# Attention and two MoE layers on one core: a longer transfer latency in the ordering model, own slots for the last old sums, and new early priorities

## The chip, the cores and the metric

The kernel runs on one core of one Trainium2 chip. The metric is the device time of one execution in microseconds. Three runs of the kernel before gave 543.34, 543.43 and 543.93 us; the median is 543.43 us.

## What is computed

Causal attention over 2 batches, 12 heads, 448 positions and head size 64, then two feed-forward blocks on the 896 tokens. Weights arrive in 64-bit floats for the matrices, and the work is done in pairs of fp32r parts (a high and a low part, three matmuls for one product).

```python
def reference(**kwargs):
    ...
    attn_out = _attn_ref(**attn_kwargs)              # softmax(q k^T / 8, causal) v
    x = np.ascontiguousarray(attn_out.transpose(0, 2, 1, 3)).reshape(B * S, H * D)   # 896 x 768
    x = _moe_ref(x=x, **moe_kwargs)                  # ((x w1) * (x w2)) w3 w_out
    return _moe2_ref(x=x, **moe2_kwargs)             # h = x w_in;  (h * clip(h + 3, 0, 6) / 6) w_out
```

Sizes: w1 and w2 are 768 x 1024, w3 is 1024 x 1024, the first w_out 1024 x 768, w_in 768 x 2048, the second w_out 2048 x 768.

## The kernel before

**Stages.** (1) Attention in 12 units (batch, pair of heads): scores (`s`, L539), the running minimum (`max`, DVE L551), exponent (`exp`, ACT L555), scaling (POOL L574), transposes (`ptp`, L597) with their copy out (ACT L602), product with v (`o`, L614). Beside it the product w3 w_out (`pw`, L683, 16 banks of 24 matmuls of 384 columns), which goes to DRAM (`product_of`). (2) `pa` (L831): x w1 and x w2 by Strassen's seven products. (3) `px` (L947): (a * b) times the product of stage 1. (4) eight `pg` groups (L831; x2 w_in, hard swish, 63 matmuls each) with `po` groups between them (`collected`, L1083, 48 matmuls each), whose partial sums go to DRAM and come back (`sums_of`: stored at L798, loaded at L1078). (5) `joined`: the last three `po` groups, 42 matmuls each by Strassen's products, which load the old sums once more (L1042), add (L1046) and store the output (L1050).

**Weights.** A unit of 64-bit weights is fetched by SP (`fetch`, L331, into `raw`, `raw2` or a slot beside), and turned into fp32r parts by `convert`: `bits` (ACT L361, ACT L364 or DVE L368, DVE L371), in Strassen groups `combine` (DVE L439), and `split` (ACT L341 or POOL L337, DVE L343).

**The order.** Every operation is an entry of `Plan` with an engine, a cost, what it reads and writes, and a rank. `Plan.issue` plays the entries through a small model of the engines: an operation is ready when what it needs has ended, plus a latency (0.2 us behind PE, 2.4 us behind a transfer on SP), and each engine takes the ready operation of lowest rank. The order so found is the order in each engine's instruction stream; on the chip each engine executes its stream in that order and waits at whatever is not there yet. PE also prefers to stay with the kind of its last operation for `RUN[kind]` operations. In attention the rank is the unit's number plus an offset of `RANK`; the fetch of weight unit n has rank `PACE * n`, its conversion `PACE * n + 1` up to the last unit of w3 (n = 15; units 0, 5, 6 are w3, 1 to 4 and 7 to 10 w_out, 11 to 15 w3). The `pw` products have rank 50 and up; late stages have `DENSE + n`, with `AHEAD` = 2.39 on top for a conversion. The evictions of `pw` have rank `EVICT`, the sums that `pa` needs (`difference`, `moving`) rank `FORM`. `FILL` = 60 transposes of nothing (L640) have rank 1000 and go where the model sees PE with nothing else.

**Slots of the last part.** `joined(i)` loads four tiles of old sums, o[m, b]. In groups i = 0 and 2 they take slots of the tags `c22` (b = 0) and `a2` (b = 1), two slots each; in group 1 of `a1` and `r`. `collected` takes `c22` and `a2` for its own sums. A slot is free when the tile that held it has been stored. The tiles `T1_0` to `T2_2` of `tp` hold the moving operands of `pg` and are last read by the eighth `pg` group.

Of the kernel before, what the change touches and what calls it, by code (L numbers as in the profile page):

```python
# [16 lines left out]

RANK = {'load': -0.56, 'max': -1.83, 'exp': -9.0, 'pt': 0.3, 'pv': 1.3}  # L20

BANKS = {'s': 3, 'pt': 2, 'o': 1}
DENSE_BANKS = 2
# [3 lines left out]
AHEAD = 2.39  # L27

BESIDE = 50.0
PACE = 0.74  # L30

EVICT = -8.56

POOLED = ("wr", "w3")
DENSE = 100.0
# [12 lines left out]

ASIDE = 48

THIRD = 0.969 * 2.0 ** -29, -0.26

FORM = -7.3

WARM = 13

LATER = 2.97

UP = 1

# [1 line left out]

FILL, IDLE = 60, 1000.0

RUN = {'r': 4, 'f': 7, 'q': 11}
TURN = {("q", "f"): 0.17, ("q", "r"): 0.15, ("q", "c"): 0.1, ("f", "q"): 0.09, ("r", "q"): 0.09, ("c", "q"): 0.1, ("f", "r"): 0.1, ("f", "c"): 0.09, ("r", "c"): 0.09, ("c", "f"): 0.17, ("c", "r"): 0.15}
SHAPE = (2, 12, 448, 64)
DFF, DFF2 = 1024, 2048
# [20 lines left out]
class Plan:  # L89
# [8 lines left out]
    def __init__(self):  # L98
        self.ops = []
        self.tags = {}  # L100
        self.ports = set()
        self.kinds = {}

    def tile(self, make, tag, bufs, after=()):
        return Handle(self, make, tag, bufs, after)
# [24 lines left out]
    def issue(self):  # L130
        n = len(self.ops)
        deps = [set(o[3]) for o in self.ops]
        order = set()
        for bufs, hs in self.tags.values():
            for x, h in enumerate(hs):
                first = h.uses[0][0]
                if x >= 1:
                    before = hs[x - 1].uses[0][0]
                    if before not in deps[first]:
                        order.add((before, first))  # L140
                    deps[first].add(before)
                if x >= bufs:
                    deps[first].update(u[0] for u in hs[x - bufs].uses)
                deps[first].update(h.after)
                deps[first].discard(first)
                for u in h.uses:
                    if u[0] != first:
                        if first not in deps[u[0]]:
                            order.add((first, u[0]))
                        deps[u[0]].add(first)  # L150
        after = [[] for _ in range(n)]
        for i in range(n):
            for j in deps[i]:
                after[j].append(i)
        left = [len(d) for d in deps]
        ready = [0.0] * n
        engines = {o[0] for o in self.ops}
        coming = {e: [] for e in engines}
        here = {e: [] for e in engines}
        free = {e: self.START.get(e, 0.0) for e in engines}  # L160
        for i in range(n):
            if not left[i]:
                heapq.heappush(coming[self.ops[i][0]], (0.0, i))
        busy, locked = None, 0.0

        def settle(i, end):
            e = self.ops[i][0]
            for j in after[i]:
                near = self.ops[j][0] == e and (e != "sp" or (i, j) in order)
                ready[j] = max(ready[j], end + (self.CHAIN.get(e, 0.0) if near else self.LATENCY.get(e, 0.15)))  # L170
                left[j] -= 1
                if not left[j]:
                    heapq.heappush(coming[self.ops[j][0]], (ready[j], j))

        kind, run = "f", 0
        todo = n
        while todo or busy:
            t, e = min((
                (free[e] if here[e] else max(free[e], coming[e][0][0]), e)
                for e in engines if here[e] or coming[e]  # L180
            ), default=(float("inf"), None))
            if busy and busy[1] <= t:
                settle(*busy)
                busy = None
                continue
            while coming[e] and coming[e][0][0] <= t:
                i = heapq.heappop(coming[e])[1]
                heapq.heappush(here[e], (self.ops[i][4], i))
            same = [x for x in here[e] if self.kinds[x[1]] == kind] if e == "pe" and run < RUN.get(kind, 0) else None
            if same:  # L190
                i = min(same)[1]
                here[e].remove(min(same))
                heapq.heapify(here[e])
            else:
                i = heapq.heappop(here[e])[1]
            self.ops[i][2]()
            todo -= 1
            cost = self.ops[i][1]
            if e == "pe":
                cost += TURN.get((kind, self.kinds[i]), 0.0)  # L200
                run = run + 1 if kind == self.kinds[i] else 1
                kind = self.kinds[i]
            if e == "pool":
                free[e] = max(t, locked) + cost
                busy = i, free[e]
                continue
            free[e] = t + cost
            if i in self.ports:
                locked = free[e]
                if busy:  # L210
                    free["pool"] = busy[1] + cost
                    busy = busy[0], free["pool"]
            settle(i, free[e])
        return max(free.values())


@with_exitstack
def attention_moe_moe2(ctx: ExitStack, tc, q, k, v, w1, w2, w3, w_out, v_in, v_out, out):
# [683 lines left out]
    second(KF - 1)  # L902

    x2 = {}

    def differences(p, ps, rank):

# [123 lines left out]
    def joined(i):  # L1031
# [1 line left out]
        n = first_of["po", c, i]  # L1033
        rank = DENSE + n
        X, Y, Z = (dense_bank(f"po{a}{i}") for a in "XYZ")
        o = {}
        for m in (0, 1):
            for b in range(B):
                name = f"o{c}_{m}_{b}_{i}"
                o[m, b] = scratch(("a2", "r")[i % 2], name) if b else scratch("a1", name) if i % 2 else spare(name)  # L1040
                t, at_ = o[m, b], (i + HK * m, b)
                plan.op("sp", 0.6, lambda t=t, at_=at_: nc.sync.dma_start(t[:, :], sums_of[at_]),  # L1042
                        reads=[summed.at(at_)], writes=[t], rank=rank - 2)

        def add(x, bank, stored=None):
            plan.op("dve", dve(S), lambda: nc.vector.tensor_tensor(x[:, :], bank[:, :S], x[:, :], ALU.add),  # L1046
                    reads=[bank], writes=[x], rank=rank)
            if stored:
                m, b = stored
                plan.op("sp", 0.6, lambda: nc.sync.dma_start(  # L1050
                    out[(i + HK * m) * P:(i + HK * m + 1) * P, cols(b)], x[:, :]), reads=[x], rank=rank)

        multiply(i, "P1", X, True, rank, "vo")
        add(o[0, 0], X)
        multiply(i, "P2", Y, True, rank, "vo")
        add(o[0, 0], Y, (0, 0))
        multiply(i, "P6", X, False, rank, "vo")
        add(o[0, 1], X)
        multiply(i, "P5", Z, True, rank, "vo")
        add(o[1, 1], Z)  # L1060
        multiply(i, "P7", X, False, rank, "vo")
        add(o[1, 1], X, (1, 1))
        multiply(i, "P3", Z, False, rank, "vo")
        add(o[0, 1], Z, (0, 1))
        multiply(i, "P4", X, False, rank, "vo")
        add(o[1, 0], X, (1, 0))

    def collected(c, i):
        n = first_of["po", c, i]
# [90 lines left out]
```

## Time and profile before

| | |
|---|---|
| median of three runs | 543.43 us |
| the profiled execution | 544.48 us, its span 542.6 us |
| PE busy | 530.2 us (98%) |
| DVE, ACT, POOL busy | 409.3, 306.0, 114.6 us |
| DMA | 87.18 MB, 161 GB/s over the span |

The span is the time from the first to the last instruction of the program in one profiled execution; some 1.9 us lie around it. PE is TensorE, PEld its weight loads, DVE VectorE, ACT ScalarE, POOL GpSimd, SPq the queue of SyncE, which here issues every transfer. PE counts as busy from the start to the modelled end of a matmul, and matmuls overlap, so a busy share near 100% can hide a slow rate: the starts of successive matmuls tell the rate. In a row of the timeline the bracket tells how long the engine had been idle before the instruction, and what ended that.

### The profile page before, as it was taken

Reading aid. Unit: us, or ns where it says so; the run is one execution under the profiler, and the core shown is the slowest. Engines: PE = TensorE matmul, PEld = TensorE weight load, DVE = VectorE, ACT = ScalarE, POOL = GpSimd, SP = SyncE. Lnnn points to the kernel's source line nnn. Section 1 sums busy time; section 2 is a strip of 40 time slices with the busy share of each in tenths; the row PEclk is TensorE's granted clock in tenths of the full one; section 3 lists DMA queues with packets and bytes.
Section 4 is the critical chain, followed back from the end, with each engine's and each line's share of the span. In section 5 each row is a group of like instructions: output and inputs, shape, how many; then the busy total and the mean of one; then the engine's idle time right before and its main releaser. Section 6 shows DMA issues by size and latency. Waiting matters only on the chain.

```text
span 542.6 us, 8387 instructions
## 1 busy us (share of the span) xinstructions
PE 530.2 (98%) x3031; PEld 468.4 (86%) x3031; DVE 409.3 (75%) x780; ACT 306.0 (56%) x597; POOL 114.6 (21%) x156
## 2 busy tenths in 40 slices
PE   9999999999999999999999999998999999999997
PEld 6657777778999999999999999997999889999886
DVE  4998989464686888987555678997757795899564
ACT  4787878776634555645434257986646542576000
POOL 3767874443021111110000120101020000000000
PEclk9999999999999999999999999998999999999999
DMA  7877775431422333333412105545563747462763
GB/s 253 307 231 231 303 240 205 156 98 30 151 62 110 116 117 126 144 125 132 175 37 80 56 4 185 220 158 165 185 210 127 267 165 233 171 209 88 229 198 131
DMA packets 33513, 87.18 MB, mean 161 GB/s; under 512 B 3264, under 2 KB 23488, under 8 KB 30912
## 3 DMA queue, kind: packets, MB, share of 16 engines
q1 hardware_dynamic: 33472, 86.65, 46.9%
q8 instruction: 23, 0.38, 0.3%
q14 instruction: 18, 0.15, 0.1%
HBM read 72.48 MB, written 14.16 MB: 160 GB/s over the span
## 4 chain that ended last, share of the span: by engine, by line
PE 71%; DVE 13%; ACT 7%; DMA 6%; issue 2%; POOL 1%; SPq 0%; DVEq 0%; POOLq 0%; ACTq 0%
PE pw L683 11%; PE px L947 11%; PE paX L831 11%; PE po L1083 10%; PE pgX L831 5%; PE paZ L831 5%; PE o L614 3%; PE paY L831 3%; PE s L539 3%; PE ptp L597 2%; PE pgZ L831 2%; DVE prb L551 2%; PE poX L831 2%; DMA vor<-in_moe_w_out 2%; DMA sums_of<-o 1%
## 5 line engine op out<-in xcount | busy, mean ns | idle before, releaser
L1083 PE MATMUL po<-g,vo 128*128 128x448 f32 x432 | 87.4, 362 | 0.0
L1083 PEld LDWEIGHTS po<-g,vo 128*128 128x128 f32 x432 | 81.0, 187 | 5.4
L683 PE MATMUL pw<-wr,w 128*128 128x384 f32 x384 | 73.3, 343 | 0.1
L683 PEld LDWEIGHTS pw<-wr,w 128*128 128x128 f32 x384 | 65.5, 188 | 7.2 <-issue 6.1
L574 POOL TENSOR_SCALAR prb<-prb,sums 128x64 f32<-128x64 f32 (+6 forms) x84 | 56.7, 692 | 44.4 <-DVE sums L568 24.6
L947 PE MATMUL px<-ab,wp 128*128 128x448 f32 x288 | 57.8, 362 | 0.0
L947 PEld LDWEIGHTS px<-ab,wp 128*128 128x128 f32 x288 | 54.0, 187 | 3.6
L555 ACT ACTIVATE prb<-prb,sums 128x64 f32<-128x64 f32 (+6 forms) x84 | 42.1, 502 | 21.1 <-DVE sums L551 20.6
L337 POOL TENSOR_SCALAR vja<-vir 128x768 fp32r<-128x768 f32 x8 | 9.1, 1134 | 166.5 <-DVE x2t L770 53.0
L551 DVE CUSTOM_DVE_ANT_0 prb<-s,maskb 128x64 f32<-128x64 f32 (+6 forms) x84 | 32.0, 415 | 12.7 <-PE s L539 11.2
L602 ACT COPY pt<-ptp 128x512 f32<-128x512 f32 x48 | 26.2, 585 | 8.9 <-PE ptp L597 8.8
L539 PE MATMUL s<-ks,qs 64*64 64x192 f32 (+6 forms) x336 | 30.3, 406 | 0.4 <-DVE sums L551 0.4
L597 PE MATMUL ptp<-ident,prb 128*128 128x128 f32 x120 | 24.7, 278 | 1.2 <-ACT pt L602 0.6
L775 ACT ACTIVATE rab<-q,consts 128x448 f32<-128x448 f32 x24 | 16.2, 674 | 16.1 <-DVE q L975 16.0
L614 PE MATMUL o<-pt,vr 128*64 128x448 f32 (+3 forms) x192 | 23.4, 386 | 0.0
L794 DVE TENSOR_TENSOR o<-po,o 128x448 f32<-128x448 f32 x24 | 14.9, 622 | 9.6 <-PE po L1083 4.7
L614 PEld LDWEIGHTS o<-pt,vr 128*64 128x64 f32 x192 | 12.7, 136 | 10.7 <-issue 5.5
L361 ACT ACTIVATE vor<-vor 128x1024 f32<-128x1024 f32 x12 | 14.0, 1164 | 13.3 <-DMA vor<-in_moe_w_out 13.3
L337 POOL TENSOR_SCALAR w2b<-w2r 128x768 fp32r<-128x768 f32 x8 | 9.3, 1165 | 54.4 <-DVE w2r L439 22.5
L597 PEld LDWEIGHTS ptp<-ident,prb 128*128 128x128 f32 x120 | 15.7, 140 | 4.4 <-ACT pt L602 1.4
L831 PE MATMUL pgX<-T3g,vjb 128*128 128x448 f32 x72 | 17.0, 384 | 2.5 <-ACT q L972 2.5
L597 PE MATMUL ptp<-swap,prb 128*128 128x128 f32 x72 | 18.0, 277 | 0.9 <-ACT pt L602 0.8
(184 smaller groups left out, 1181.5 us busy)
## 6 DMA issues: line engine op xcount, KB each, us to landing
vor<-in_moe_w_out SPq DMA_DIRECT2D x12, 1024.0 KB, 5.5
w3r<-in_moe_w SPq DMA_DIRECT2D x8, 1024.0 KB, 5.3
sums_of<-o SPq DMA_DIRECT2D x36, 224.0 KB, 3.0
o<-sums_of SPq DMA_DIRECT2D x36, 224.0 KB, 3.0
wrr<-in_moe_w_out SPq DMA_DIRECT2D x8, 768.0 KB, 6.4
w1r<-in_moe_w SPq DMA_DIRECT2D x8, 768.0 KB, 5.9
w2r<-in_moe_w SPq DMA_DIRECT2D x8, 768.0 KB, 4.4
vjr<-in_moe_w_in SPq DMA_DIRECT2D x8, 768.0 KB, 4.4
```

Source lines behind the costliest of these rows:

```text
L337: plan.op("pool", single(size), lambda: nc.gpsimd.tensor_scalar(hl[:, HI, at_:at_ + size], x(), 1.0, 1.0, ALU.mult, ALU.mult), reads=reads ...
L539: nc.tensor.matmul(ps[at_:at_ + T, :n], qs[u][T * j:T * j + T, t * T:(t + 1) * T], ks[u][T * j:T * j + T, :n], start=True, stop=True)
L551: plan.op("dve", dve(n), lambda: nc.vector.tensor_tensor_reduce(out=z(), in0=ps[:, :n], in1=maskb[:, S - n:], scale=-SCALE, scalar=3.0e38, ...
L555: plan.op("act", 0.29 + n * 0.00083, lambda: nc.scalar.activation(z(), z(), AF.Exp, bias=sm[:, 0, t:t + 1], scale=-1.0, accum_out=sm[:, 1, ...
L574: nc.gpsimd.tensor_scalar(s, s, sm[:, 1, t:t + 1], 1.0, ALU.mult, ALU.mult)
L597: nc.tensor.transpose(ps[:, i * P:(i + 1) * P], pb[:, OFF[t] + kb * P:OFF[t] + (kb + 1) * P], swap if t % 2 else ident)
L602: plan.op("act", act(4 * P), lambda: nc.scalar.copy(d[:, 4 * g:4 * g + 4].rearrange("p n h i -> p (n h i)"), ps[:, :]), reads=[ps], writes ...
L614: nc.tensor.matmul(ps[T * j:T * j + T, kb * P:S], vr[u][:, kb, j, :], d[:, base[kb]:base[kb] + TQ - 2 * kb, j, :], start=kb == 0, stop=kb ...
L683: nc.tensor.matmul(ps[:, :W], weight(n, a, kk), hls[m][:, c, at_:at_ + W], start=kk == 0 and a == c, stop=kk == KF - 1 and a == LO)
L831: nc.tensor.matmul(ps[:, :S], hl[:, a, off + kk * P:off + (kk + 1) * P], t[:, c, at_], start=first and kk == 0 and a == c, stop=kk == n - ...
L947: nc.tensor.matmul(ps[m, b][:, :S], weight(n, a, kk), ab[kk][:, c, cols(b)], start=kk == 0 and a == c, stop=kk == KF - 1 and a == LO)
L1083: nc.tensor.matmul(ps[:, :S], hls[n][:, a, at_:at_ + P], gt[k][:, d, cols(b)], start=kk == 0 and a == d, stop=kk == KC - 1 and a == LO)
```

## The change

Three things. In `Plan.issue`, a transfer on SP among the operations made after `plan.dense` (set behind the last `pa` group, so from `px` on) makes its dependents ready 4.0 us (`SLOW`) after its end in the model, where the latency was 2.4 us; what only follows in the SP queue's order keeps its rule. `joined` takes for its old sums the slots `T2_i` (m = 0) and `T1_i` (m = 1), each [P, 2, S] with the two batches side by side. And eight constants of the early part have new values: ranks in attention, `PACE`, `EVICT`, `FORM`, `LATER` (the rank of the loads of v), and `RUN`. The arithmetic, and the number of matmuls, are the same.

```diff
-RANK = {'load': -0.56, 'max': -1.83, 'exp': -9.0, 'pt': 0.3, 'pv': 1.3}
+RANK = {'load': -0.54, 'max': -3.0, 'exp': -7.72, 'pt': 0.75, 'pv': 1.25}
-PACE = 0.74
-EVICT = -8.56
+PACE = 1.21
+EVICT = -9.28
+SLOW = 4.0
-FORM = -7.3
+FORM = -14.03
-LATER = 2.97
+LATER = 3.56
-RUN = {'r': 4, 'f': 7, 'q': 11}
+RUN = {'r': 5, 'f': 6, 'q': 19}
...
+        self.dense = 1 << 30
...
                 near = self.ops[j][0] == e and (e != "sp" or (i, j) in order)
+                if e == "sp" and i >= self.dense and not near:
+                    ready[j] = max(ready[j], end + SLOW)
...
     x2 = {}
+    plan.dense = len(plan.ops)
...
-        o = {}
+        o = [plan.tile(lambda a=a: later["t"].tile([P, 2, S], F32, tag=f"{a}_{i}", name=f"o{c}_{a}_{i}"), f"{a}_{i}", 1, (done,))
+             for a in ("T2", "T1")]
         for m in (0, 1):
             for b in range(B):
-                name = f"o{c}_{m}_{b}_{i}"
-                o[m, b] = scratch(("a2", "r")[i % 2], name) if b else scratch("a1", name) if i % 2 else spare(name)
-                t, at_ = o[m, b], (i + HK * m, b)
-                plan.op("sp", 0.6, lambda t=t, at_=at_: nc.sync.dma_start(t[:, :], sums_of[at_]),
-                        reads=[summed.at(at_)], writes=[t], rank=rank - 2)
-
-        def add(x, bank, stored=None):
-            plan.op("dve", dve(S), lambda: nc.vector.tensor_tensor(x[:, :], bank[:, :S], x[:, :], ALU.add),
-                    reads=[bank], writes=[x], rank=rank)
+                plan.op("sp", 0.6, lambda t=o[m], b=b, at_=(i + HK * m, b): nc.sync.dma_start(t[:, b, :], sums_of[at_]),
+                        reads=[summed.at((i + HK * m, b))], writes=[o[m].at(b)], rank=rank - 2)
+
+        def add(m, b, bank, stored=False):
+            t = o[m]
+            plan.op("dve", dve(S), lambda: nc.vector.tensor_tensor(t[:, b, :], bank[:, :S], t[:, b, :], ALU.add),
+                    reads=[bank], writes=[t.at(b)], rank=rank)
...
         multiply(i, "P1", X, True, rank, "vo")
-        add(o[0, 0], X)
+        add(0, 0, X)
...
```

The other calls of `add` change in the same way.

## Rows read from the trace of the kernel before

**Rows 1.** Stretch: length, busy us (count) of PE, PEld, DVE, ACT, POOL; PEclk, DMA, GB/s.
```profile
0.00:57.00 57.00, 53.13 (x420) 36.20 (x421) 45.81 (x127) 41.82 (x110) 37.63 (x62) 1.00 0.76 261
...
370.00:380.00 10.00, 7.77 (x32) 6.75 (x31) 7.55 (x11) 5.96 (x9) 1.93 (x2) 0.83 0.34 112
```
**Rows 2.** Chain that ended last, stretches of one kind: start us, us, what.
```profile
116.48 1.88 PE o L614 x16
...
119.26 2.29 PE pw L683 x12
...
126.86 1.88 PE o L614 x16
...
138.82 21.00 PE pw L683 x120
...
260.61 57.60 PE px L947 x288
```
**Rows 3.** Timeline of the tail: start us, us, engine, line, tiles, [idle before].
```profile
510.96 1.36 PE L831 MATMUL poX<-g,voa 128*128 128x448 f32 x6
...
521.11 1.48 PE L831 MATMUL poZ<-g,voc 128*128 128x448 f32 x6 [1.10 <-DVE o L1046]
```
**Rows 4.** The chain in the tail.
```profile
514.05 2.84 DMA sums_of<-o
516.91 3.40 DMA o<-sums_of
...
537.65 1.22 PE poX L831 x6
```
**Rows 5.** Timeline around 375 us, PE and ACT.
```profile
371.08 1.97 PE L831 MATMUL pgZ<-T1g,vjb 128*128 128x448 f32 x9
...
373.63 1.18 ACT L361 ACTIVATE vor<-vor 128x1024 f32<-128x1024 f32 x1 [2.75 <-DMA vor<-in_moe_w_out]
...
375.29 3.17 PE L831 MATMUL pgX<-T3g,vjb 128*128 128x448 f32 x9 [2.23 <-ACT q L972]
...
382.38 1.96 PE L1083 MATMUL po<-g,vo 128*128 128x448 f32 x9
```
**Rows 6.** Timeline around 433 us, PE and ACT.
```profile
429.19 1.97 PE L831 MATMUL pgZ<-T1g,vjb 128*128 128x448 f32 x9
...
430.06 0.90 ACT L361 ACTIVATE vjr<-vjr 128x768 f32<-128x768 f32 x1 [1.08 <-DMA vjr<-in_moe_w_in]
...
437.74 3.56 PE L1083 MATMUL po<-g,vo 128*128 128x448 f32 x17
```
**Rows 7.** The chain at these two places: start us, us, what.
```profile
365.33 8.22 DMA vor<-in_moe_w_out
...
422.65 7.33 DMA vjr<-in_moe_w_in
```
**Rows 8.** Time to landing of the twelve vor transfers, 256 to 543 us.
```profile
DMA to landing us min/median/max: 4.7/5.5/8.2
```
**Rows 9.** PE's groups from 4.3 to 57 us: shapes, count, busy us, mean ns.
```profile
L539 PE MATMUL s<-ks,qs 64*64 64x128 f32 (+6 forms) x156 | 15.4, 423 | 0.4 <-DVE sums L551 0.4
...
L683 PE MATMUL pw<-wr,w 128*128 128x384 f32 x48 | 10.0, 350 | 0.1
...
L614 PE MATMUL o<-pt,vr 128*64 128x448 f32 (+3 forms) x64 | 7.8, 386 | 0.0
```
**Rows 10.** ACT's main groups in the first 60 us, columns as in rows 9.
```profile
L555 ACT ACTIVATE prb<-prb,sums 128x256 f32<-128x256 f32 (+6 forms) x39 | 19.9, 511 | 12.4 <-DVE sums L551 12.2
...
L602 ACT COPY pt<-ptp 128x512 f32<-128x512 f32 x20 | 10.9, 586 | 2.5 <-PE ptp L597 2.5
...
L361 ACT ACTIVATE wrr<-wrr 128x768 f32<-128x768 f32 x8 | 7.4, 930 | 0.0
...
L555 ACT ACTIVATION_READ_ACCUMULATOR prb<-prb,sums 128x1 f32 x39 | 7.3, 188 | 0.0
```

More of the change, by code (lines that the diff above doesn't have):

```diff
@@ L1048, in add @@
             if stored:
-                m, b = stored
                 plan.op("sp", 0.6, lambda: nc.sync.dma_start(
-                    out[(i + HK * m) * P:(i + HK * m + 1) * P, cols(b)], x[:, :]), reads=[x], rank=rank)
+                    out[(i + HK * m) * P:(i + HK * m + 1) * P, cols(b)], t[:, b, :]), reads=[t.at(b)], rank=rank)
         multiply(i, "P1", X, True, rank, "vo")
-        add(o[0, 0], X)
+        add(0, 0, X)
         multiply(i, "P2", Y, True, rank, "vo")
-        add(o[0, 0], Y, (0, 0))
+        add(0, 0, Y, True)
@@ L1057, in joined @@
         multiply(i, "P6", X, False, rank, "vo")
-        add(o[0, 1], X)
+        add(0, 1, X)
         multiply(i, "P5", Z, True, rank, "vo")
-        add(o[1, 1], Z)
+        add(1, 1, Z)
         multiply(i, "P7", X, False, rank, "vo")
-        add(o[1, 1], X, (1, 1))
+        add(1, 1, X, True)
         multiply(i, "P3", Z, False, rank, "vo")
-        add(o[0, 1], Z, (0, 1))
+        add(0, 1, Z, True)
         multiply(i, "P4", X, False, rank, "vo")
-        add(o[1, 0], X, (1, 0))
+        add(1, 0, X, True)
```

## The prediction

> **What bounds the kernel now.** I read the page first (engines, the 40 slices), then the chain that ended last, then busy time by stretch, then the timeline where PE had waited. PE is busy for 98% of the span, and the chain runs through PE for nearly all of the time from 57 to 330 us. So the question at each place is not who is busy but whether PE is fed at full rate, and the starts of matmuls tell that: 288 `px` matmuls of 448 columns take 57.60 us, 0.20 us each, and 120 `pw` matmuls take 21.00 us, 0.175 us each [rows 2]. The work of PE is the same before and after, so the change can only give back time in which PE ran below these rates. I find four such places.
>
> The tail: the three `joined` groups begin at 510.96 and the last matmul ends at 537.65 + 1.22 = 538.87 [rows 3, 4]. That is 27.9 us for 126 matmuls; at 0.20 us they need 25.2. Lost: 2.7 us. The chain shows why: a store of old sums takes 2.84 us, a load of old sums follows it for 3.40 us, DVE adds, and PE waits for the bank [rows 3, 4].
>
> Around 375 us: PE should have begun its next product 1.80 us after 371.08 and, three products of 1.80 us later, the `po` group at 378.3; it began at 382.38 [rows 5]. Lost: 4.1 us. ACT stood 2.75 us at the conversion of `vor`, and the copy that frees PE's bank was queued behind it. PE waited 2.23 us; then its clock, 0.83 over this window [rows 1], made the next nine matmuls take 3.17 us where 1.97 us is the row of an undisturbed nine [rows 5].
>
> Around 433 us, the same with a shorter wait: 429.19 + 4 x 1.80 = 436.39, begun at 437.74 [rows 6]. Lost: 1.35 us, at full clock. ACT stood 1.08 us at `vjr` with the copy behind it.
>
> The first 57 us: PE did some 5 units of attention (64 `o` matmuls are 4 units, 156 `s` matmuls 5.6) and 48 `pw` matmuls [rows 9]. At full rate one unit with two runs of 12 `pw` takes 126.86 - 116.48 = 10.38 us [rows 2], less 24 x 0.175 = 4.2: 6.2 us for the unit. So 5 x 6.2 + 8.4 = 39.4 us of the 52.7 us from 4.3 us on were useful, 13.3 us were lost (19 if I count 4 units, 10 if 5.6). The 60 filling transposes lie in there. From 57 us until `pw` ends PE has no such gap.
>
> **The change part by part.**
>
> *Own slots.* Before, group 0 of `joined` loads into `c22` and `a2`, behind the stores of the last `collected` group, which has the same slots. The last of these stores lands at 514.05 + 2.84 = 516.89, and the load starts at 516.91 [rows 4]. Now the slots are those of the moving operands of the eighth `pg` group, which are last read some 25 us before `joined` begins. The data of group 0 was stored some 20 us before. So the loads of groups 0 and 1 can land early. Group 2 really needs the last stores: 516.9 plus 3.4 us is 520.3, and its turn on PE comes at 511 + 2 x 8.4 = 527.8, so 7 us of cover remain. The loads now stand earlier in SP's queue, among the fetches and the stores of sums; a load that waits there for a store (up to about 3 us) holds what is queued behind, but by then the last weights are already issued, and the output stores behind it have no reader. What is late next is PE's own order, with one bank copied out during the next product of 1.2 us. Value: -2.7 us, with bounds -2.7 and 0.
>
> *A latency of 4.0 us.* The model gives a transfer its cost on SP (0.0035 us per column, 3.58 us for `vor`, 2.69 us for `vjr`) plus the latency. The old model expected `vor` 5.98 us after its start; it took 8.22 us [rows 7]. Put on the chip's clock, in the old model it lands at 371.3. The copy is ready when the product that ran up to the next one's start at 371.08 [rows 5] has drained and the model's 0.2 us are over, at about 371.5. So ACT took the conversion first. In the new model it lands 7.58 us after, at 372.9, 1.4 us behind the copy: ACT does the copy first, and PE goes on. That is -4.1 us, with bounds -4.1 and 0 (the model's clock need not run with the chip's). For `vjr` the new model says 6.69 us against 7.33 us [rows 7], that is 429.3; the copy for which PE waited is ready at about 429.4. This is a tie; I take half, -0.7 us, with bounds -1.35 and 0. A conversion that comes later in the order costs nothing as long as ACT or DVE has other work and the unit is needed only one group later (8 to 12 us of PE); if that cover goes, PE waits for weights, and the dearest row for such a wait is the 4.1 us. The whole late order is drawn anew by this, so I put in one new wait of the kind at 433 us, +1.4 us. Bounds for new waits: 0 and two of the kind at 375 us, +8.2.
>
> A rule speaks against the 4.0. The Trainium skill ("DMA: Bandwidth & Descriptors", Anatomy of one DMA) gives a transfer a constant part of about 2.0 us. By that rule 2.4 was already enough, the new figure only delays conversions in the order, and the value of this part would be 0. The trace agrees for the usual transfer: the median `vor` landed after 5.5 us [rows 8], 1.9 us over its cost. It differs for the two that hurt: 8.22 - 3.58 = 4.6 us and 7.33 - 2.69 = 4.6 us.
>
> *Early priorities.* `PACE` from 0.74 to 1.21 is the large one. Conversion n had rank 0.74 n + 1 beside units 0 to 11, and now has 1.21 n + 1: the fifth conversion, with which the first `pw` can run, goes from rank 4.0 to 5.8, the eleventh from 8.4 to 13.1, behind all of attention. `max` at -3.0 pushes DVE the same way. So attention goes ahead and `pw` starts later; fetches move with their conversions on SP, behind the loads of q, k and v. What attention alone gives PE is limited by ACT: per unit seven exponents with their reads, (19.9 + 7.3) / 39 x 7 = 4.9 us, and four copies, 2.2 us [rows 10], with one conversion of 0.93 us [rows 10] some 8.0 us, in which PE has 6.2 us of attention. The loss is 1.8 us per unit until `pw` fills it: for some 6 units 11 us, and some 3 us of start. That is 14 us against the 13.3 us before: 0, with bounds -4 (a loss of 9 us, near the smaller count above) and +13 (attention starves PE through all 12 units, 22 us, and 4 us of start). DVE's 45.8 busy us of 57 [rows 1] say the same: DVE has little left for more.
>
> *`RUN` r from 4 to 5.* A run of 12 `pw` matmuls takes 2.29 us [rows 2] where 12 x 0.175 is 2.10: 0.19 us for the turn. After 57 us, beside attention, 384 - 48 - 120 = 216 matmuls go in 18 runs; in runs of 15 they are 14.4. 3.6 x 0.19 = -0.7 us, with bounds -0.7 and +0.5 (a transpose held up by the longer run, 3 x 0.175 us once). The other numbers (f, q, `EVICT`, `FORM`, `exp`, `pt`, `pv`, `load`, `LATER`) exchange neighbours: an eviction or a forming step of half a microsecond before or behind another on ACT and DVE, hidden by products of 4.2 us in two banks; v comes 0.6 ranks later, and PE showed no wait at `o` [rows 9]. 0, with bounds -0.5 and +0.5.
>
> Sum: -2.7 - 4.1 - 0.7 + 1.4 + 0 - 0.7 = -6.8 us. The profiled execution took 544.48 us (span 542.6 and 1.9 around), 1.05 us over the median of 543.43; on the median the sum gives 536.6, on a profiled execution like this one 537.7.
>
> **The rivals.**
>
> *Only the tail.* The late order moves its waits rather than losing them, because the usual transfer was modelled well [rows 8]. Then -2.7 us remain: 540.7. For it: each long landing sits where the DMA was crowded, and a new order crowds other places. Against it: the wait at 375 us hangs on an order decided by 0.2 us.
>
> *Early starvation.* The slower side. Place: 30 to 110 us. PE finds neither attention nor `pw`, since the conversions are behind attention on DVE and ACT. Price: up to +13 us as above; it turns the sign when the early loss goes past 13.3 + 6.8 = 20 us, and PE's clock, which fell after 2.23 us of waiting at 375 us [rows 1, 5], would make it dearer. With all 13: 543.4 + 13 - 6.8 = 549.6; at the middle between sign change and worst 546.5. For it: ACT needs 8.0 us for what PE does in 6.2. Against it: DVE and ACT have some 2.5 us free per unit, which is nearly one conversion.
>
> *Early gain.* Attention ahead fills PE better: the early loss falls to 9 us, and the sum is -10.8: 532.6. For it: the fillers show idle time that real work could take. Against it: ACT's limit.
>
> *The change does not do what it says.* The gains are eaten by an early loss of 6 to 8 us: 543.4, within 0.2%.
>
> **How the numbers follow.** Forecast (536.6, from 534.5 to 539) 0.42; only the tail (540.7) 0.20; early gain (532.6) 0.10; no change 0.10; slower (546.5) 0.18. About 0.2%, 1.1 us, is what a measurement of this kernel can tell from no change. Faster 0.72, same 0.10, slower 0.18. The range takes in the early gain and the first half of the slower case: 532 to 545.5.
>
> **What would show it.** Tail: `joined` in 25.2 us, its loads issued long before 511 us, no idle time of PE there. Late: no row in which ACT stands for a transfer with a copy of a bank behind it, PEclk 1.00 in all slices behind 320 us. Early: attention ends before 136 us, the last `pw` ends within 4 us of 159.65; more `pw` matmuls in a row (15). The prediction is wrong if `pa` starts later than 166 us, or if new waits behind 260 us add up to more than 4 us.

## The result and the profile after

The changed kernel takes 538.01 us (median of 4 runs, 537.39 to 539.07) beside 543.38 us for the kernel before (4 runs, 543.02 to 543.93): a ratio of 0.9902, with a 95% interval of 0.9883 to 0.9922. That is 5.4 us faster; 6.8 were forecast. In a later comparison on one chip with other kernels it gave 537.70 us beside 542.16, a ratio of 0.9924 (0.9895 to 0.9953), which is 4.5 us by the medians. Of the twelve runs of the changed kernel with the old latency (below), one took 1343.36 us and is left out of its median and its ratio.

The profiled execution took 538.42 us with a span of 536.3, against 544.48 and 542.6 before. The page of the kernel after, its first lines and the clock row of its 40 slices:

```profile
span 536.3 us, 8389 instructions
...
PE 527.3 (98%) x3031; PEld 466.9 (87%) x3031; DVE 408.9 (76%) x780; ACT 304.7 (57%) x597; POOL 121.0 (23%) x156
...
PEclk9999999999999999999999999999999999999999
```

PE executes 3031 matmuls as before. Its busy time fell from 530.2 to 527.3 us, so 2.9 of the 6.3 us of span were matmuls that had taken longer, and the other 3.4 us are time in which PE had stood. The starts of the first matmul of each stage on PE's timeline, in the two profiled executions, tell in which stage. `pa`, `pg` and `joined` are the starts; the end is that of the last matmul.

| | before | after | difference of the stretch that ends there |
|---|---|---|---|
| `pa` starts | 159.65 | 159.49 | -0.16 |
| `pg` starts | 318.05 | 317.89 | 0.00 |
| `joined` starts | 510.96 | 507.05 | -3.75 |
| last matmul ends | 538.87 | 532.60 | -2.36 |

The tail first. These are lines of the timeline after (start us, us, engine, line, operation, tiles, idle before), and the last step of the chain on PE:

```profile
504.43 1.40 SPq L1046 DMA_DIRECT2D o_T<-sums_of  x3
...
507.05 1.36 PE L836 MATMUL poX<-g,voa 128*128 128x448 f32 x6
...
517.94 1.45 PE L836 MATMUL poX<-T2o,voc 128*128 128x448 f32 x6
...
531.39 1.21 PE poX L836 x6
```

The first three loads of `joined` are issued 2.6 us ahead of its first matmul, where before the load started at 516.91 behind a store [rows 4]. From 507.05 to 531.39 + 1.21 = 532.60 are 25.55 us, against 27.9 before [rows 3, 4] and 25.2 at full rate. The 1.10 us for which PE waited for DVE before [rows 3] has no counterpart.

Around 375 us, the timeline after on PE, ACT and DVE:

```profile
371.65 0.52 ACT L978 COPY q<-pgX 128x448 f32<-128x448 f32 x1
...
373.18 1.96 PE L836 MATMUL pgX<-T3g,vjb 128*128 128x448 f32 x9
...
374.40 1.19 ACT L366 ACTIVATE vor<-vor 128x1024 f32<-128x1024 f32 x1 [0.48 <-DMA vor<-in_moe_w_out]
...
375.87 1.37 DVE L373 TENSOR_SCALAR vor<-vor 128x1024 uint32<-128x1024 uint32 x1
377.16 0.60 DVE L981 TENSOR_TENSOR q<-q,pgX 128x448 f32<-128x448 f32 x1
377.82 2.08 PE L836 MATMUL pgX<-T4g,v 128*128 128x448 f32 x9 [0.87 <-DVE q L981]
...
379.73 3.56 PE L1087 MATMUL po<-g,vo 128*128 128x448 f32 x17
```

ACT now copies PE's bank out (371.65) before it turns to `vor` (374.40), and the 2.23 us wait and the slow nine matmuls of 3.17 us [rows 5] are gone. A smaller wait of 0.87 us has come at 377.82, this time for DVE: the add that frees the bank (377.16) stands behind a step of `vor` that DVE began at 375.87. Behind the start of `pg` the list of what PE waited for (us in total, times, longest) names only this one and a short one at 326 us:

```profile
PE pgX L836 <- DVE q L981: 0.9, 1, 0.9
PE pgX L836 <- DVE T2g L932: 0.3, 1, 0.3
```

Early, the chain shows the new runs of `pw`, and the end of attention:

```profile
126.52 2.61 PE pw L688 x15
...
132.61 1.88 PE o L619 x16
134.49 25.16 PE pw L688 x144
159.65 1.80 PE paX L836 x9
```

Attention ends at 134.49, where before it ended at 138.82 [rows 2]. But 144 `pw` matmuls are left over instead of 120, and `pa` starts where it did.

### The profile page after: what moved, and what is told of

The parts are those of the page before. It is cut to its first block, busy times and chain, and to the rows that moved or that the text cites. A ratio compares the mean times of both kernels' runs of the same rounds, so it can differ in the third digit from the quotient of the medians.

```text
span 536.3 us, 8389 instructions
## 1 busy us (share of the span) xinstructions
PE 527.3 (98%) x3031; PEld 466.9 (87%) x3031; DVE 408.9 (76%) x780; ACT 304.7 (57%) x597; POOL 121.0 (23%) x156
## 4 chain that ended last, share of the span: by engine, by line
PE 78%; DVE 13%; ACT 4%; DMA 1%; issue 1%; POOL 1%; POOLq 0%; DVEq 0%; ACTq 0%
PE po L1087 14%; PE paX L836 11%; PE px L953 10%; PE pw L688 9%; PE pgX L836 7%; PE paZ L836 5%; PE pgZ L836 4%; PE poX L836 3%; PE paY L836 3%; PE o L619 3%; PE s L544 2%; PE ptp L602 2%; PE pgY L836 2%; DVE prb L556 2%; PE poZ L836 1%; DMA wrr<-in_moe_w_out 1%
## 5 line engine op out<-in xcount | busy, mean ns | idle before, releaser
L579 POOL TENSOR_SCALAR prb<-prb,sums 128x64 f32<-128x64 f32 (+6 forms) x84 | 63.0, 769 | 42.5 <-ACT prb L560 24.2
L688 PE MATMUL pw<-wr,w 128*128 128x384 f32 x384 | 72.2, 342 | 0.1
L342 POOL TENSOR_SCALAR w2a<-w1r 128x768 fp32r<-128x768 f32 x8 | 7.6, 954 | 53.6 <-PE paZ L836 30.7
L792 DVE SCALAR_TENSOR_TENSOR g<-rab,g 128x448 fp32r<-128x448 f32 x28 | 17.0, 617 | 2.0 <-ACT g L790 2.0
```

The source lines that it names most:

```text
L342: plan.op("pool", single(size), lambda: nc.gpsimd.tensor_scalar(hl[:, HI, at_:at_ + size], x(), 1.0, 1.0, ALU.mult, ALU.mult), reads=reads ...
L579: nc.gpsimd.tensor_scalar(s, s, sm[:, 1, t:t + 1], 1.0, ALU.mult, ALU.mult)
L688: nc.tensor.matmul(ps[:, :W], weight(n, a, kk), hls[m][:, c, at_:at_ + W], start=kk == 0 and a == c, stop=kk == KF - 1 and a == LO)
```

## The experiments

The theory, as predicted: the time is won in two places, by the slots in the tail and by one exchange in ACT's order around 375 us; the early part is worth nothing. The rivals: only the tail counts, since the usual landing was modelled well; or the early priorities move the time, to either side. In each group below the kernels share their runs of the kernel before. Stretches are between starts on PE's timeline, as in the table above; from `pg` to `joined` the least that the full rate allows is 187.2 us (eight groups of 12.6, nine of 9.6). The last column of stretches ends at the start of the last add on DVE.

### The parts, one at a time

Slots alone, on the kernel before:

```diff
-        o = {}
+        o = [plan.tile(lambda a=a: later["t"].tile([P, 2, S], F32, tag=f"{a}_{i}", ...), f"{a}_{i}", 1, (done,))
+             for a in ("T2", "T1")]
...
```

> The kernel before with the own slots alone. Theory (the three parts act apart, each at its place): the joined groups take some 25.5 us instead of 27.9, everything up to 510 us stays, about 541.0 us (-2.4). Rival (the gain of the tail needs the longer latency too, since the loads must also stand early in SP's order): no idle time of PE is saved in the tail, 543.4 us. Rival (the new slots draw a new late order): the waits around 375 and 433 us change as well, anything from 537 to 545 us.

Latency alone, with `joined` and the early numbers as before:

```diff
+SLOW = 4.0
...
+                if e == "sp" and i >= self.dense and not near:
+                    ready[j] = max(ready[j], end + SLOW)
...
+    plan.dense = len(plan.ops)
```

> The kernel before with the longer latency alone. Theory: the waits of PE around 375 us (4.1 us lost) and 433 us (1.35 us) go, some 1.5 us of new small waits come, the tail keeps its 2.7 us: about 539.5 us (-4). Rival (these waits went in the changed kernel because the new early order shifted the model's clock, not because of the latency): they stay, 543.4 us or a little to either side.

Early numbers alone:

```diff
-PACE = 0.74
+PACE = 1.21
...
-RUN = {'r': 4, 'f': 7, 'q': 11}
+RUN = {'r': 5, 'f': 6, 'q': 19}
...
```

> The kernel before with the new early constants alone (ranks, PACE, EVICT, FORM, LATER, RUN). Theory: the first pa product starts at 159.65 us as in both kernels, the late stages follow shifted by nothing, 543.4 us (0). Rival (the early order decides the late waits): the waits at 375 and 433 us go although the latency is the old one, 538 to 540 us.

Slots and latency together, with the early numbers of before:

```diff
-PACE = 1.21
+PACE = 0.74
...
-RUN = {'r': 5, 'f': 6, 'q': 19}
+RUN = {'r': 4, 'f': 7, 'q': 11}
...
```

> The changed kernel with the early constants of before: longer latency and own slots. Theory: the two gains add, 537 to 538 us, like the changed kernel, since the early part gave nothing. Rival (the early order matters for the late waits): 540 us or more.

Measured, against 541.72 us for the kernel before in the same comparison:

| kernel | us | ratio (95%) | `pa` starts | `pg` to `joined` | `joined` to its last add |
|---|---|---|---|---|---|
| before (first profile) | | | 159.65 | 192.91 | 27.93 |
| slots | 539.12 | 0.9963 (0.9941 to 0.9985) | 159.81 | 191.45 | 25.91 |
| latency | 545.35 | 1.0068 (1.0042 to 1.0095) | 158.69 | 189.20 | 32.92 |
| early | 541.46 | 0.9986 (0.9962 to 1.001) | 158.61 | 191.25 | 26.92 |
| slots and latency | 537.75 | 0.9936 (0.9913 to 0.996) | 158.40 | 189.14 | 25.58 |

The slots give the tail its 2 us by themselves, and slots and latency together give what the whole change gives within the intervals. The early numbers alone can't be told from no change. The surprise is the latency alone, for which 539.5 us were expected: it wins nearly 4 us between `pg` and `joined` as it should, and loses 5 in the tail, so that it ends slower than before. The chain of that kernel shows a large part of the loss (start us, us, what):

```profile
530.31 2.58 DMA o<-sums_of
...
533.70 2.44 PE poX L836 x6
536.14 1.83 PE poZ L836 x6
```

and its timeline at this place:

```profile
529.23 0.62 DVE L1052 TENSOR_TENSOR o<-poY,o 128x448 f32<-128x448 f32 x1 [0.24 <-PE poY L836]
...
530.31 1.36 SPq L1048 DMA_DIRECT2D o<-sums_of  x3
...
533.02 0.62 DVE L1052 TENSOR_TENSOR o<-poX,o 128x448 f32<-128x448 f32 x1 [3.16 <-DMA o<-sums_of]
...
533.70 2.44 PE L836 MATMUL poX<-T3o,voa 128*128 128x448 f32 x6 [1.92 <-DVE o L1052]
```

Three loads of old sums for the last group are issued only at 530.31. In the new order they stand on SP behind an output store, and that store waits for the add of 529.23. DVE then waits 3.16 us for the load and PE 1.92 us for DVE, and the next six matmuls take 2.44 us where 1.36 is an undisturbed six. In all PE waits 4.8 us for DVE in this tail, and about 1.9 in the tail before. With slots of its own this stretch takes 25.58 us with the same latency. So the parts are not additive: the late order of the change is only good on top of the new slots.

### Is it the one exchange?

The changed kernel with the old latency everywhere, the changed kernel unaltered, and its latency at 3.0:

```diff
-    plan.dense = len(plan.ops)
```

> The changed kernel with the latency of 2.4 us in the late stages too (own slots and early constants stay). In ACT's order the conversion of vor stands again ahead of the copy of the bank. Theory: the wait of PE around 375 us is back, 1 to 2.2 us idle and up to 4 us lost, the tail stays at 25.6 us: 540 to 541.5 us, 2 to 4 us over the changed kernel. Rival (the late waits left with the early order, not with the latency): as the changed kernel, 538 us.

> The changed kernel as it is, once more beside the kernel before on the chip of this job, so that the others can be held against it. All theories: 537 to 539 us, 0.7 to 1% under the kernel before.

```diff
-SLOW = 4.0
+SLOW = 3.0
```

> The changed kernel with a late latency of 3.0 us. ACT's order has the first copy ahead of the conversion of vor and the second behind it. Theory (what matters is which of the two stands first in the order, and a transfer that lands later than the model says): most of the 4 us at 375 us stay away, the second copy has 1.8 us of cover, so 538 to 540 us. Rival (the latency must cover the slow landings in full): 540 to 541.5 us, as with 2.4.

The kernel of the slots alone, in which the model takes a latency of 4.0 for one single transfer, the `vor` that landed late:

```diff
+            if (name, m) == ("vo", 1):
+                plan.slow = j
...
+                if i == self.slow and not near:
+                    ready[j] = max(ready[j], end + 4.0)
```

> The kernel before with own slots, and with the longer latency for a single transfer alone: the load of vor that lands around 373.6 us. Up to there the order of all engines is that of the kernel with own slots; there ACT takes the copy of the bank before the conversion. Theory: the wait of PE around 375 us goes with this one exchange, 3 to 4 us less than own slots alone, 535.5 to 537.5 us. Rival (the stall only moves to the next product, since the conversion then comes later): no gain over own slots alone, 539 us.

Against 542.16 us for the kernel before in this comparison:

| kernel | us | ratio (95%) | `pg` to `joined` | `joined` to its last add | the group at 375 us |
|---|---|---|---|---|---|
| after, unaltered | 537.70 | 0.9924 (0.9895 to 0.9953) | 189.10 | 25.57 | 13.70 |
| after, old latency | 540.46 | 0.9962 (0.9936 to 0.9988) | 190.43 | 25.75 | 15.04 |
| after, latency 3.0 | 538.85 | 0.9940 (0.9919 to 0.996) | 187.48 | 29.69 | 12.60 |
| slots, one transfer | 537.65 | 0.9922 (0.9896 to 0.9948) | 187.93 | 26.40 | 13.13 |

The changed kernel's first profile had 13.75 in the last column, which is the time from the first matmul of the `pg` group in which `vor` arrives to the start of its `po`; 12.6 is the full rate, 16.69 was before, 16.61 with the slots alone. With the old latency the order and the wait are back, as the timeline of that kernel shows:

```profile
372.08 1.20 ACT L366 ACTIVATE vor<-vor 128x1024 f32<-128x1024 f32 x1 [2.66 <-DMA vor<-in_moe_w_out]
373.15 0.55 ACT L977 COPY q<-pgX 128x448 f32<-128x448 f32 x1
...
373.75 2.08 PE L836 MATMUL pgX<-T3g,vjb 128*128 128x448 f32 x9 [2.16 <-ACT q L977]
```

With the one transfer told to be slow, it is gone:

```profile
370.96 0.53 ACT L977 COPY q<-pgX 128x448 f32<-128x448 f32 x1 [0.45 <-PE pgX L836]
...
372.52 1.96 PE L836 MATMUL pgX<-T3g,vjb 128*128 128x448 f32 x9
...
373.11 1.17 ACT L366 ACTIVATE vor<-vor 128x1024 f32<-128x1024 f32 x1 [1.14 <-DMA vor<-in_moe_w_out]
```

The transfer itself took as long in both (8.09 and 8.08 us on their chains), and 8.08 us with the slots alone, from which the last kernel differs at this place only in where ACT and DVE take `vor` in their order. So the exchange takes the wait away, and not an earlier landing. Of the 4 us, 0.5 stay, since the next copy on ACT stands behind the same conversion. The slots and this one exchange give the ratio of the whole change, 0.9922 beside 0.9924. That settles the mechanism at 375 us. Beside the slots alone, the median is 1.5 us lower and not the 3 to 4 us that were expected; the two stood in different comparisons.

The latency of 3.0 is the best of all between `pg` and `joined` (187.48, 0.3 us over the full rate: the exchange without the new waits at 326 and 378 us), and loses more than that, 4.1 us, in the tail. Its timeline there:

```profile
507.71 0.63 DVE L799 TENSOR_TENSOR o<-po,o 128x448 f32<-128x448 f32 x1 [2.27 <-DMA o<-sums_of]
508.25 0.61 DVE L1051 TENSOR_TENSOR o_T<-poX,o_T 128x448 f32<-128x448 f32 x1
...
508.92 2.06 PE L836 MATMUL poX<-T2o,voc 128*128 128x448 f32 x6 [1.99 <-DVE o_T L1051]
...
510.78 2.40 PE L836 MATMUL poZ<-T1o,voa 128*128 128x448 f32 x6
```

It is the pattern of 375 us on another engine: DVE stands 2.27 us for a load, and the add that frees a bank of PE is queued behind it. PE waits 1.99 us and then runs two sixes in 2.06 and 2.40 us instead of 1.36.

### Weights and sums told apart, and the early part

If the model's latency for weights decides the middle and the one for old sums decides the tail, they should want different values. Weights cost more than 1.5 us in the model, sums 0.6. First 4.0 for weights and the old latency for sums, then 3.0 for weights and 4.0 for sums:

```diff
-                if e == "sp" and i >= self.dense and not near:
+                if e == "sp" and i >= self.dense and self.ops[i][1] > 1.5 and not near:
```

> The changed kernel with the longer latency for the transfers of weights alone; the loads and stores of partial sums keep 2.4 us in the model. The late order up to some 480 us stays nearly the same. In the tail DVE's order has the last add of a collected group ahead of the adds that free the banks of the first joined group, as with 3.0 us for all. Theory (PE waits wherever an engine stands for a transfer with the copy of a bank behind it): no wait around 375 us, but 2 to 4.5 us lost in the tail: 540 to 542 us. Rival (the long latency is needed for the weights only): 537.5 us as the changed kernel.

```diff
-                    ready[j] = max(ready[j], end + SLOW)
+                    ready[j] = max(ready[j], end + (3.0 if self.ops[i][1] > 1.5 else SLOW))
```

> The changed kernel with a late latency of 3.0 us for weights and 4.0 us for partial sums. Theory (order alone counts, place by place): the stretch from pg to joined as with 3.0 us for all, 187.5 us instead of 189.1, and the tail as in the changed kernel, 25.6 us: 536 us, 1 to 1.5 us under the changed kernel. Rival (each new set of numbers draws new waits at random): 538 to 541 us.

For the early part, the changed kernel without its 60 filling transposes, and with conversions ranked far behind attention:

```diff
-FILL, IDLE = 60, 1000.0
+FILL, IDLE = 0, 1000.0
```

> The changed kernel without the 60 filling transposes (0.11 us each, 6.6 us of PE in the first 26 us). The results are the same, the fillers' are not used. Theory (PE waits there for softmax and conversions anyway, and ACT and DVE set the pace): pa starts at 158 to 160 us as with them, 537 to 539 us; if the clock falls in the gaps it is 1 to 3 us more. Rival (the fillers take time from real work): up to 4 us less.

```diff
-PACE = 1.21
+PACE = 3.0
```

> The changed kernel with PACE at 3.0, so that the conversions of weights stand behind nearly all of attention. It measures the price of starving pw of weights. Theory of the prediction (ACT needs 8.0 us for an attention unit in which PE has 6.2 us of work; the gap is lost until pw can fill it): attention ends by 110 us, and pa starts 5 to 13 us later than 159 us: 543 to 551 us. Rival (where the conversions stand hardly matters, since engines take what is ready): pa within 2 us of 159 us, 538 us.

Against 541.70 us for the kernel before in this comparison, on another chip:

| kernel | us | ratio (95%) | `pa` starts | `pg` to `joined` | `joined` to its last add |
|---|---|---|---|---|---|
| 4.0 for weights only | 538.57 | 0.9936 (0.9911 to 0.9961) | 158.40 | 189.14 | 25.74 |
| 3.0 weights, 4.0 sums | 536.87 | 0.9906 (0.9881 to 0.9931) | 158.19 | 187.64 | 25.81 |
| no filling transposes | 535.63 | 0.9886 (0.9857 to 0.9915) | 156.56 | 189.14 | 25.57 |
| `PACE` 3.0 | 537.17 | 0.9922 (0.9895 to 0.995) | 158.88 | 189.14 | 25.58 |

*Weights only.* Expected was a loss in the tail, and there was none. The order has the same weak point as the one with 3.0, with the last `collected` add ahead of the first adds of `joined` on DVE; but here the load had landed, and DVE waited for PE instead:

```profile
506.22 0.62 DVE L799 TENSOR_TENSOR o<-po,o 128x448 f32<-128x448 f32 x1 [1.85 <-PE po L1087]
```

So the order in the tail is an exposure (a loss that comes only when a transfer lands late): it cost 4 us where the load was late, and nothing where it was not.

*3.0 and 4.0.* Both stretches are good at once, as the theory wants: 187.64 and 25.81. The profiled execution is 2.5 us below the first of the change (535.91 and 538.42 us) and 0.5 below its second (536.39); by medians it is 1.7 us below its neighbour with weights only in the same comparison. Its ratio lies inside the interval of the change, so that it beats the change is shown by the stretches of one profile and not by the ratios.

*`PACE` 3.0.* The starvation of PE that was the slower rival does not come. In the first 57 us (columns as in [rows 1], and then PE's group of `pw` as in [rows 9]):

```profile
0.00:57.00 57.00, 53.68 (x441) 37.47 (x442) 45.86 (x140) 45.24 (x121) 39.50 (x63) 1.00 0.80 271
...
L688 PE MATMUL pw<-wr,w 128*128 128x384 f32 x60 | 12.6, 351 | 0.5 <-DVE w L348 0.5
```

With conversions ranked behind all of attention, PE had 60 `pw` matmuls done by then, more than the 48 of before [rows 9] and than the 48 and 55 of the change in its two profiles. Attention did not go ahead either: its last `o` run begins at 137.06, beside 132.54 in the change. The ranks only decide between works that are ready at once, and it seems that DVE and ACT still find time for conversions while attention waits for its own steps. That reason is argued; that `pa` starts at 158.88 is measured (three of its matmuls, 0.6 us, ran ahead at 145.80).

*No filling transposes.* The theory expected 537 to 539 us; it took 535.63. Without them the granted clock drops early, and still `pa` starts at 156.56, the earliest of all kernels. Windows of that kernel and its group of `pw` from 4.3 to 57 us, then the same of the changed kernel (a clock of 1.00 is 2.4 GHz; a stretch between 0.50 and 1.00 ran partly at 1.2):

```profile
0.00:10.00 10.00, 6.16 (x46) 3.99 (x50) 4.43 (x22) 5.96 (x16) 3.75 (x21) 1.00 0.77 273
10.00:20.00 10.00, 9.74 (x59) 4.45 (x61) 7.40 (x25) 7.04 (x20) 7.31 (x10) 0.66 0.69 245
0.00:57.00 57.00, 51.50 (x390) 33.36 (x391) 45.50 (x142) 43.68 (x120) 38.98 (x64) 0.94 0.79 272
...
L688 PE MATMUL pw<-wr,w 128*128 128x384 f32 x65 | 13.3, 349 | 0.0
```
```profile
0.00:10.00 10.00, 8.64 (x58) 6.02 (x59) 2.90 (x16) 3.76 (x12) 3.01 (x18) 1.00 0.78 270
10.00:20.00 10.00, 8.98 (x83) 5.94 (x82) 9.30 (x28) 8.16 (x24) 6.78 (x9) 1.00 0.76 245
0.00:57.00 57.00, 53.38 (x441) 36.62 (x441) 45.72 (x139) 43.66 (x119) 40.15 (x63) 1.00 0.79 264
...
L688 PE MATMUL pw<-wr,w 128*128 128x384 f32 x48 | 10.2, 352 | 0.1
```

Without fillers PE is busy for 6.16 of the first 10 us instead of 8.64, and the clock of the next 10 us is 0.66 instead of 1.00. All the same PE has done 65 `pw` matmuls by 57 us instead of 48 (55 in the second profile of the change), with as many `o` and `s` (64 and 176) as with them. About 1 us is lost again between `pa` and `pg` (159.49 us against 158.40), where PE waited 0.8 us for ACT. It has the lowest median of all kernels that were run. The interval of its ratio overlaps that of the change; in its own comparison five of its six runs (534.53 to 537.31) lie below all six with `PACE` 3.0 (536.84 to 539.54), a kernel that also differs from the change in the early part alone. So the fillers, which keep the clock up, cost more than they save: some 1.5 to 2 us by medians (537.17 - 535.63; 537.70 for the change in its comparison on the other chip). The profiles show less of it for certain: `pg` starts at 316.05 without fillers, and at 317.89 and 316.27 in the two of the change. To put this together with 3.0 and 4.0 was not tried.

## Why the prediction was nearly right

Term by term, on the profiled executions, where 6.8 us were forecast and 6.3 of span were found.

**Slots: -2.7 forecast, -2.36 found.** The step holds: loads issued ahead of `joined`, no wait of PE of 0.2 us or more. Left are 0.35 us over the full rate. With the slots alone the tail is nearly as short (25.91), so the term belongs to them. What the prediction called hidden, the loads' new place in SP's queue, is hidden only with this slot choice: with the shared slots the same latency gave 32.9 us.

**Latency at 375 us: -4.1, found as -4.1 with a new wait of 1.15 us beside it.** The group went from 16.69 to 13.75 us. The order was decided where the prediction put it, by the copy against a `vor` modelled too early, and one altered transfer reproduced it. The part of it that was the clock is not fixed: with the kernel before and the slots alone, a wait of 2.23 and of 2.13 us was followed by a clock of 0.83 [rows 1, 5]; with the old latency on the changed kernel a wait of 2.16 us, and with the early numbers alone one of 2.41 us, was followed by full clock, and the group lost 2.4 and 2.7 us instead of 4.1. Windows of 370 to 380 us of the slots alone and of the changed kernel with the old latency:

```profile
370.00:380.00 10.00, 7.87 (x32) 6.90 (x31) 7.68 (x11) 5.93 (x9) 1.92 (x2) 0.83 0.37 121
```
```profile
370.00:380.00 10.00, 7.84 (x39) 7.00 (x39) 8.71 (x13) 6.87 (x12) 1.74 (x2) 1.00 0.17 69
```

So this exchange takes away a loss of 2.4 to 4.1 us, by execution. The granted clock of the single runs, a mean over the whole run, agrees. Where ACT has the old order here (the kernel before, the slots, the early numbers, the old latency), it was 0.997 or less in 40 of 95 runs, and these runs of a kernel were on average 1.8 to 2.7 us longer than its others. With the exchange and the slots it never was, in 42 runs of the change, of slots and latency, of the one transfer, of weights only, of 3.0 and 4.0 and of `PACE` 3.0. The other kernels are not counted: the latency alone and the latency of 3.0 can lose clock in the tail, and the kernel without fillers early. Where in a run the clock fell is known for the profiled ones alone.

**433 us: -0.7, found -1.35, but for another reason in part.** The slots alone have the same order on ACT as before, the conversion of `vjr` ahead of the copy, and lost nothing, since `vjr` had landed. Its timeline:

```profile
428.96 0.91 ACT L361 ACTIVATE vjr<-vjr 128x768 f32<-128x768 f32 x1
...
429.77 0.51 ACT L972 COPY q<-pgX 128x448 f32<-128x448 f32 x1
...
436.46 1.76 PE L1081 MATMUL po<-g,vo 128*128 128x448 f32 x8
```

The loss before [rows 6] was one of its own execution. In the seven profiles with the old order here, `vjr` landed after 7.3, 7.1, 6.6, 6.1, 6.1, 5.5 and 5.2 us (before, early, old latency, slots, one transfer, 3.0 and 4.0, latency 3.0). The group lost 1.35, 1.1 and 0.6 us in the first three and nothing in the others. The changed kernel has the copy ahead (427.33, the conversion at 428.20), `vjr` landed after 6.7 us, and nothing was lost. The prediction counted every loss of one profile as a property of the kernel; this one was an exposure to a late landing.

**New waits: +1.4, found +1.7** (1.15 at 375 us, the rest mostly at 326 us), none of the dear kind. The prediction had put one wait at 433 us, where none came, so that the size fits is luck. The latency of 3.0 has neither, so they are the price of 4.0 and not of the idea.

**Early: 0 and -0.7, found -0.2.** In seven profiles with the new early numbers `pa` starts from 157.87 to 159.49, in five with the old ones from 158.40 to 159.81. The means are 158.5 and 159.2: 0.7 us apart, which is the term for the longer runs, and no more than the scatter, since the unaltered change alone gave 159.49 and 157.87. So it may be there, and is not shown. The value 0 was right by luck, its working was not: it set a loss of 14 us against 13 from ACT's 8.0 us per unit against PE's 6.2, and put 0.18 on starvation. `PACE` 3.0 should have made that loss far worse, and did not. What sets the early time is not shown.

**The signs.** Of what was named as signs, `joined` took 25.55 us for 25.2, the clock is full behind 320 us, attention ended before 136 us, the last `pw` ended at 159.65, and runs of 15 `pw` are seen. Two signs came only in part. The first loads of `joined` were issued 2.6 us ahead of it, not long before. And ACT still stands once for a transfer with a copy next in its order (5.24 us for a `vor` until 451.29), where PE's bank was not ready yet and nothing was lost. Neither of the two limits (`pa` later than 166, new waits over 4 us) was met.

**The median.** The forecast went from 544.48 down to 537.7 for such an execution and 536.6 for the median; found were 538.42 and 538.01. The kernel before was profiled 1.1 us above its median, the kernel after 0.4. Over all comparisons the kernel before ran from 538.8 to 545.8 us, and kernels with the exposed order at 375 us spread widely (the slots alone 537.75 to 542.74), those with the exchange less (one transfer 536.47 to 538.27, the change 537.39 to 539.07 and 536.39 to 538.34). The losses that were removed happen in full only in part of the executions; a sum made from one execution in which all of them were there is too high for the gain in the median. So 6.8 us were forecast, 6.1 were found between the two profiled executions, and 4.5 to 5.4 between medians.

Of the rivals, "only the tail" falls with the one transfer (1.5 us of median, and the group 3.5 us shorter, beside the slots alone), "early starvation" with `PACE` 3.0, "early gain" with the early numbers alone, which can't be told from no change. The prediction set the rule of the Trainium skill ("DMA: Bandwidth & Descriptors", Anatomy of one DMA), a constant part of about 2.0 us, against the latency of 4.0 and said that the trace agrees for the usual transfer. The twelve late `vor` after the change have

```profile
DMA to landing us min/median/max: 4.7/5.6/7.8
```

a median of 5.6 - 3.58 = 2.0 us over the cost in the kernel's model. That bears out the model's 2.4 for the median transfer, but it did not decide: the transfer that hurts is the late one. It does not bear out the rule as it stands. The section of the Trainium skill gives the 2.0 us for transfers that GpSimd issues, and adds to them the bytes at 436 GB/s; for 1024 KB that is an estimate of 4.4 us. Here SP issues every transfer, and each of the twelve took longer, 4.7 us at the least.

## What to carry to other kernels

In an order fixed ahead for engines that run strictly in turn, look for a step that waits for a transfer with a step that frees a matmul bank queued behind it; a latency in the model that puts the freeing step first is enough. For weights 3.0 us did best here, between the median's 2.0 and the 4.6 us of the late landings; for old sums 4.0 gave the safe order in the tail, and 3.0 and 2.4 did not. So set the figure for each kind of transfer. A loss read from one profile is a fixed cost or an exposure; only other executions tell which. Of a change in several parts, one part can be slower alone, because another takes away what it would collide with.

## What was not expected of the hardware

The same transfer was late in nearly every kernel: `vor` at 365 us took 8.22 us before, and 8.08, 8.39, 8.09 and 8.08 us in four others (slots, early, old latency, one transfer), where the median is 5.5. In 13 of 14 profiles it took 7.8 to 8.5 us, and in one (weights only) 5.9. So a late landing goes with the place in the stream of transfers, but is not certain there. The queue's share of the DMA engines' time does not decide it alone: from 360 to 375 us it was 82.5% in the kernel of weights only and 81.4% in that of slots and latency, in which the same `vor`, issued at the same 365.37, took 7.8 us. The landing of `vjr` at 422 us varied from 5.2 to 7.3 us.

At 375 us a wait of PE of 2.13 and 2.23 us was followed by a granted clock of 0.83 in two profiles, and one of 2.16 and 2.41 us by 1.00 in two others, with nearly the same work around it. In the tails of the latency alone and of the latency of 3.0, waits of 1.92 and 1.99 us were followed by six matmuls in up to 2.44 and 2.40 us. So the length of the wait did not decide; what does was not found. And without fillers a stretch of 10 us at 0.66 early in the kernel cost less than the 60 transposes that avoid it, by the medians above.
